# Block products for f tiles 8 to 11 of the first four batches, a later load, and a rewritten opening list

## The chip, the cores and the metric

The kernel runs on one core of one Trainium2 chip. The metric is the device time of one execution in microseconds; the kernel before was timed three times, and the median is 711.96 us. A separate execution was recorded by the hardware profiler, and all rows of the trace come from it.

## The reference

Eight batches of attention over 32 learned memory slots, followed by a gated feed-forward layer over all tokens:

```python
a = exp(phi - max(phi, -2)); a = a / (sum(a, -2) + 1e-9)       # over the sequence
k_m, v_m = einsum(a, k), einsum(a, v)                          # 32 slots a head
attn = softmax(q @ k_m.T / 8) @ v_m                            # batch, head, 576, 64
x = attn.transpose(0, 2, 1, 3).reshape(4608, 512)
out = (sigmoid(x @ w_gate) * (x @ w_val)) @ w_out              # d_ff = 1536
```

All data is float32, and the result is held to float32 accuracy.

## The kernel before

**Tiles.** A batch b has S = 576 rows. The hidden width 1536 is cut into NFT = 12 tiles f of 128. Rows are cut in two halves c: c = 0 has 256 rows, c = 1 has 256 rows and a tail of 64. The tails of two batches (a pair) are put together to one tile of 128 rows in the tiles `left`.

**Two terms a number.** Most matmuls are split: an operand is written as hi + lo, both in the format fp32r, and a product takes three matmuls, hi by hi, hi by lo and lo by hi. So each matrix product below is three instructions on TensorE.

**The gate.** x is never formed. `make_u` multiplies v_m by the weights (tiles `u_hi`, `u_lo`, for two f at a time; it takes 16 narrow matmuls for a pair of f), and `gate_of` multiplies these by the transposed attention (`at_hi`, `at_lo`): 12 matmuls for a half of a step, six for the gate and six for the value, of 256 columns in half 0 and of 320 in half 1. ScalarE makes the sigmoid from PSUM (`curve`, L218), VectorE multiplies (L830 or L1009).

**Eight block products.** In the first scheme (`gate_half`, `out_half`, `out_of`) a finished product of 256 rows is cut to hi and lo and multiplied by w_out: two row tiles by 512 columns, three terms, six matmuls of 512 columns for a step's half (b, f, c). Two f tiles make 12 such matmuls. This is a 2 by 2 block product by the eight multiplications of the definition.

**Seven block products.** In the second scheme (`first_half`, `second_half`, `seven`, `block_product`, `merge`) a pair k of f tiles is treated as a 2 by 2 block product by seven multiplications: sums of rows are made by VectorE (L1036, L1048, L1057, and three subtractions at L233 for the low terms), sums of the weights were prepared before and lie in DRAM as `block`s of seven pieces. It takes 7 products, three terms, 21 matmuls of 256 columns. `merge` puts the accumulators together by VectorE adds (L1149 to L1152, and L1159 with the rows parked earlier).

**Order of the work.** An `OPENING` list, written out by hand, says what each engine's queue gets, up to step 19. The names: `phi`, `kvm`, `kvt`, `q`, `gate`, `out`, `more` load by SyncE's queue; `amax`, `aexp` are the first softmax; `T`, `A` turn and copy its result; `K`, `B`, `t`, `V` make keys and values; `S`, `mx`, `ms`, `ex`, `nz`, `nm`, `tp`, `hi`, `lo` are scores, second softmax and its turned hi and lo; `sz`, `bt`, `ws`, `wb`, `wh`, `wl` convert weights; `U`, `uh`, `um`, `ul` are make_u; `G`, `sg`, `gm`, `gh`, `gl`, `O`, `E`, `row` are gates, outputs and parked rows; `W n` is n matmuls of the identity that nothing reads. `step` keeps this order on each engine.

Then a loop over `steps` runs the first scheme for batches 0 to 3 (`QUAD` = 4): f 0 to 3 of each batch, then f 4 to 7, then f 8 to 11, in turns of `TURN` = 4. A turn's result is parked in DRAM (`part`) and added by the next turn's end (`out_end`, L875). The loop also converts the last weights (`CONVERT`) and makes the blocks (`prepare`). Last, batches 4 to 7 run the second scheme throughout, 12 items (n, c, k) a batch, where n is a half of the f tiles. `beside_step` places the next batch's softmax, keys and turns between (`SIDE`). `row_of` fetches a parked row over ScalarE's queue; a wait of such a fetch holds what ScalarE has behind it.

## Time and profile before

| | |
|---|---|
| median of 3 runs | 711.96 us (710.71 to 712.0) |
| the profiled execution's own time | 714.1 us |
| its span, first to last instruction | 712.3 us |
| TensorE busy | 702.2 us, 6129 matmuls |
| VectorE busy | 500.5 us, 1028 instructions |
| ScalarE busy | 391.4 us |
| GpSimd busy | 37.4 us |
| mean granted TensorE clock | 0.995 |

A busy TensorE is not yet a TensorE at its peak: matmuls overlap, and a duration is longer than the distance to the next start. What a stream of matmuls costs is read from the starts.

### The profile page before, as it was taken

What the parts mean: (1) busy time and instruction counts of PE and PEld (TensorE: products, weight loads), DVE (VectorE), ACT (ScalarE), POOL (GpSimd) and SP (SyncE); (2) the same over time, 40 slices, a digit from 0 to 9 for tenths busy, and PEclk for the clock granted to TensorE, in tenths of its full rate; (3) what the DMA queues carried; (4) which work ended last, traced back from release to release, by engine and by line L of the source; (5) the groups of instructions that cost most, each with busy time, mean ns of one, the idle gap of its engine ahead of it and who ended that gap; (6) DMA issues with size and microseconds to landing.
All of it is one profiled execution on the core that took longest, in us unless ns stands there. A gap on an engine that the chain in (4) does not pass through costs nothing.

```text
span 712.3 us, 15350 instructions
## 1 busy us (share of the span) xinstructions
PE 702.2 (99%) x6129; PEld 617.8 (87%) x6129; DVE 500.5 (70%) x1028; ACT 391.4 (55%) x883; POOL 37.4 (5%) x73
## 2 busy tenths in 40 slices
PE   8999999999999999999999999999999999999996
PEld 6778888888888978889887989898998989999996
DVE  2688777543565747679475789777886788976766
ACT  5898796555465533344553665564645455544432
POOL 0000000000000002131000000000000000000001
PEclk9999999999999999999999999999999999999999
...
GB/s 346 412 258 337 236 227 148 161 207 262 275 186 207 249 78 315 138 292 303 332 188 324 104 199 220 297 339 42 251 187 190 236 93 313 107 307 44 260 116 99
DMA packets 46631, 158.27 MB, mean 222 GB/s; under 512 B 5472, under 2 KB 14176, under 8 KB 41440
## 3 DMA queue, kind: packets, MB, share of 16 engines
...
## 4 chain that ended last, share of the span: by engine, by line
PE 96%; DMA 2%; DVE 1%; issue 0%; ACT 0%; DVEq 0%; POOL 0%; SPq 0%; ACTq 0%; POOLq 0%
PE pu_t L243 58%; PE acc L243 38%; DMA part<-left 1%; DMA q<-in_qT_dram 1%; DVE row L1245 0%; DVE g_lo L233 0%; DVE left L875 0%; DVE x L1245 0%; DVEq L1519 0%; DVE x L1009 0%; ACT g L836 0%; ACT x L218 0%; SPq L229 0%; ACTq L229 0%; DVE x L1048 0%
## 5 line engine op out<-in xcount | busy, mean ns | idle before, releaser
L243 PE MATMUL pu_t<-at_hi,u_hi 128*128 128x256 f32 (+1 forms) x760 | 224.7, 296 | 0.0
L243 PE MATMUL pu_t<-at_lo,u_hi 128*128 128x256 f32 (+1 forms) x760 | 222.6, 293 | 0.0
L243 PE MATMUL pu_t<-at_hi,u_lo 128*128 128x256 f32 (+1 forms) x760 | 222.6, 293 | 0.0
L243 PEld LDWEIGHTS pu_t<-at_hi,u_hi 128*128 128x128 f32 x760 | 142.9, 188 | 6.2 <-issue 1.2
L243 PEld LDWEIGHTS pu_t<-at_lo,u_hi 128*128 128x128 f32 x760 | 142.7, 188 | 3.1
L243 PEld LDWEIGHTS pu_t<-at_hi,u_lo 128*128 128x128 f32 x760 | 142.6, 188 | 0.0
L243 PE MATMUL acc<-wo_hi,g 128*128 128x512 f32 x384 | 135.7, 399 | 0.7 <-ACT g L836 0.7
L243 PEld LDWEIGHTS acc<-wo_hi,g 128*128 128x128 f32 x384 | 72.1, 188 | 23.2 <-issue 9.2
L218 ACT ACTIVATE sg<-pu_t 128x256 f32<-128x256 f32 x94 | 38.4, 410 | 79.7 <-PE pu_t L243 76.2
L830 DVE TENSOR_TENSOR sg<-pu_t,sg 128x256 f32<-128x256 f32 (+1 forms) x94 | 42.3, 452 | 48.3 <-ACT sg L218 32.9
L243 PE MATMUL acc<-wo_lo,g 128*128 128x512 f32 x192 | 75.2, 392 | 0.0
L233 DVE TENSOR_TENSOR g_lo<-x,g_hi 128x128 fp32r<-128x128 f32 x145 | 66.4, 463 | 11.1 <-ACT g_hi L1059 10.1
L218 ACT ACTIVATE x<-pu_t 128x320 f32<-128x320 f32 (+1 forms) x96 | 39.1, 410 | 59.9 <-PE pu_t L243 59.5
L233 DVE TENSOR_TENSOR u_lo<-pu_t,u_hi 128x512 fp32r<-128x512 f32 x92 | 57.9, 682 | 16.2 <-ACT u_hi L738 16.1
L1009 DVE TENSOR_TENSOR x<-pu_t,x 128x320 f32<-128x320 f32 (+1 forms) x96 | 43.4, 453 | 32.6 <-ACT x L218 20.6
L836 ACT CAST g<-sg 128x256 fp32r<-128x256 f32 x96 | 38.9, 405 | 34.5 <-DVE sg L830 25.4
L738 ACT CAST u_hi<-pu_t 128x512 fp32r<-128x512 f32 x92 | 48.6, 592 | 14.2 <-PE pu_t L243 13.3
L233 DVE TENSOR_TENSOR g<-sg,g 128x256 fp32r<-128x256 f32 x96 | 39.6, 420 | 22.4 <-ACT g L836 22.1
L243 PE MATMUL pu_t<-wg,vT 64*32 64x512 f32 x736 | 49.6, 598 | 0.0
L1059 ACT CAST g_hi<-x 128x512 fp32r<-128x512 f32 x47 | 29.1, 619 | 24.0 <-DVE x L1057 24.0
L243 PE MATMUL acc<-wo_hi,g_hi 128*128 128x256 f32 x220 | 40.3, 282 | 0.0
L243 PEld LDWEIGHTS acc<-wo_lo,g 128*128 128x128 f32 x192 | 36.1, 188 | 4.6
...
## 6 DMA issues: line engine op xcount, KB each, us to landing
...
ring<-block POOLq DMA_DIRECT2D x8, 1792.0 KB, 8.7
wo_hi<-block POOLq DMA_DIRECT2D x7, 1792.0 KB, 8.2
wo_lo<-block POOLq DMA_DIRECT2D x7, 1792.0 KB, 9.2
...
```

Source lines behind the costliest of these rows:

```text
L218: last_act[0] = nc.scalar.activation(*args, **kw)
L233: return nc.vector.tensor_tensor(lo, x, hi.bitcast(F32), op=ALU.subtract)
L243: last_pe[0] = do(*args, **kw)
L738: nc.scalar.copy(U[b, fs[0]][0][:, r, :nf], pb[r])
L830: last_prod[0] = nc.vector.tensor_tensor(sg, val, sg, op=ALU.mult)
L836: nc.scalar.copy(ghi, prod[:, : 2 * P].rearrange("p (j x) -> p j x", j=2))
L1009: last_prod[0] = nc.vector.tensor_tensor(x[:, :n], val, x[:, :n], op=ALU.mult)
L1059: nc.scalar.copy(gh[:, 2:6], x[:, 1:5])
```

## The change

1. The loop over `steps` ends at f 7 (`END` = 8). F tiles 8 to 11 of batches 0 to 3 run the second scheme: pairs k = 2 and 1 of the upper half n = 1 (`LATE`), 4 items a batch, 16 in all, each in place of the first scheme's two steps' halves. The row parked by the first scheme is fetched (`part_fetch`) and added in `merge`. Tails go through `left_parts` and `left_seven`.
2. Blocks are made earlier: raw sums and differences by GpSimd instead of VectorE (`block_raw`, `block_sums`), placed by half step in `PREP`; blocks 4 and 5 are made in the place where they are used first (`late_parts`) and stored later (`block_keep`). Weights w_out of f 8 to 11 aren't cut to hi and lo any more; only their sums are. Block stores go over SyncE's queue, not GpSimd's. A block is loaded by two transfers, one for hi and one for lo.
3. Keys and values of batch 6 (the seventh) are loaded in item 6 of batch 4's work, not beside the memory of batch 5.
4. The opening list is another one, and a name with ' runs its copy on the other engine (`copy`: ScalarE and VectorE change places). `W` counts 81 in all with the 24 ahead of the list, where there were 102.

The diff, cut to its core:

```diff
+END = 8
+LATE = (2, 1)
+LOW_AHEAD = {(0, 1): 4}
-PREP = [1] * 8 + [2, 1] * 6 + [1] * 20
+PREP = {
+    0: ("raw", 0), 1: ("sums", 0), 3: ("parts", 0), 4: ("raw", 1), 5: ("sums", 5), 6: ("sums", 1), 9: ("parts", 1), 10: ("parts", 5, 0), 11: ("parts", 5, 1),
+    19: ("sums", 4), 21: ("parts", 4, 0), 22: ("parts", 4, 1), 24: ("raw", 2), 25: ("put", 5), 26: ("sums", 2), 27: ("raw", 3), 28: ("sums", 3), 31: ("parts", 2), 33: ("put", 4), 35: ("parts", 3),
+}
-    21: [(8, 2)], 22: [(9, 0)], 24: [(9, 2)], 25: [(10, 0)], 27: [(10, 2)], 28: [(11, 0)], 30: [(11, 2)],
+CONVERT = {20: (10, 2), 21: (9, 0), 22: (11, 2), 24: (10, 0), 26: (8, 2), 28: (11, 0), 29: (9, 2)}
...
-phi 0; gate 0; kvm 0 0; kvt 0; kvm 0 1; amax 0; aexp 0; W 24; T 0 0; T 0 2; T 0 1; A 0 2; A 0 0; phi 1;
-q 0 0; A 0 1; W 5; K 0 0; gate 1; sz 0 1; q 0 1; out 0; gate 3; sz 0 0;  W 6; K 0 1; kvm 1 0;
-Z 0; B 0; kvt 1; amax 1; gate 2; phi 2; W 6; t 0; kvm 1 1; bt 0 1; V 0 0; aexp 1;  W 4; S 0 0;
-bt 0 0; V 0 1; Z 1; T 1 1; mx 0 0; T 1 2; sz 1; ms 0 0; W 14; S 0 1; A 1 1;  ws 0; bt 1; T 1 0;
-q 1 0; ex 0 0; mx 0 1; U 0 0; q 1 1; A 1 0; out 1; A 1 2; ms 0 1; uh 0 0; nz 0 0; ex 0 1; W 10; um 0 0;
-nm 0 0; sz 3; nz 0 1; tp 0 0; nm 0 1; hi 0 0; W 7; tp 0 1; ul 0 0; lo 0 0; K 1 0;  hi 0 1; wb 0;
...
+gate 0; sz 0 0; phi 0; kvm 0 0; kvt 0; kvm 0 1; amax 0; aexp 0; W 31; Z 0; T 0 0; A' 0 0; T 0 1; T 0 2;
+W 9; A' 0 2; A' 0 1; sz 0 1; K 0 0; phi 1; amax 1; q 0 0; gate 1; q 0 1; W 16; K 0 1; B 0; t 0; aexp 1;
+V' 0 0; bt 0 0; Z 1; bt 0 1; S 0 0; mx 0 0; V' 0 1; T 1 1; T 1 2; T 1 0; S 0 1; ms 0 0; sz 1; bt 1;
+U 0 0; W 1; mx 0 1; ms 0 1; A 1 1; A 1 0; A 1 2; ex 0 0; nz 0 0; uh 0 0; um 0 0; nm 0 0; ex 0 1; nz 0 1;
+gate 3; sz 3; tp 0 0; hi' 0 0; ul 0 0; lo 0 0; kvm 1 0; kvt 1; K 1 0; G 0 1 0; G 0 0 0; phi 2; amax 2;
+nm 0 1; out 0; ws 0; wb 0; bt 3; tp 0 1; aexp 2; sg 0 1 0; hi' 0 1; sg 0 0 0; lo 0 1; kvm 1 1; K 1 1;
+B 1; gm 0 1 0; wh 0; wl 0; gm 0 0 0; gate 2; q 1 0; q 1 1; T 2 1; T 2 0; t 1; G 0 0 1; sz 2; A 2 1;
...
+E 0 7 0 0; fetch 0 1; again 1; row 0 7 0; O 0 6 1; O 0 7 1; E 0 7 0 1; E 0 7 1 1; ul 1 6; E 0 7 1 0;
+row 0 7 2; row 0 7 1; row 0 7 3; V 4 0; V 4 1; sz 8; bt 8;
...
+    def copy(to, x, act=True):
+        (nc.scalar.copy if act != swapped[0] else nc.vector.tensor_copy)(to, x)
...
+    def block_sums(k):
+        work = works[k]
+        raw = work[:, : 2 * DM].rearrange("p (f h x) -> p f h x", f=2, h=2)
+        sums = work[:, 2 * DM :].rearrange("p (j x) -> p j x", j=4)
+        sub = lambda to, *of: nc.gpsimd.tensor_tensor(to, *of, op=ALU.subtract)
+        sub(sums[:, 1], raw[:, 0, 1], raw[:, 0, 0])
+        sub(sums[:, 0], raw[:, 0, 1], raw[:, 1, 1])
+        sub(sums[:, 2], raw[:, 1, 1], sums[:, 1])
+        sub(sums[:, 3], raw[:, 1, 0], sums[:, 2])
+    def block_raw(k):
+        work = works[k] = att([P, SF, 512], "kvm0" if k == 3 else "kvm1").rearrange("p c x -> p (c x)")
+        hi, lo = (w[:, 2 * k : 2 * k + 2, :] for w in wos)
+        nc.gpsimd.tensor_tensor(work[:, : 2 * DM].rearrange("p (f x) -> p f x", f=2), hi, lo, op=ALU.add)
...
+    def load_block(n, k, queue="stream"):
+        for i in range(2):
+            move(ring(k, i).bitcast(F32), blocks_of[n * PAIRS + k][:, i], queue)
+    def pairs(b):
+        return LATE if b < QUAD else tuple(range(PAIRS))
...
-    turns = [(b, f0, f0 + TURN) for f0 in range(0, NFT, TURN) for b in range(QUAD)]
+    turns = [(b, f0, f0 + TURN) for f0 in range(0, END, TURN) for b in range(QUAD)]
...
-        load_next(b + 1)
+        if b == QUAD + 1:
+            load_phi(b + 1)
+        else:
+            load_next(b + 1)
...
+        if late:
+            s = i % low_at
+            if s == 0 and b + 1 < QUAD:
+                again(b + 1)
+            if s in (1, 3):
+                part_fetch(b, c)
+            if b == 1 and s == 2:
+                load_block(0, 0)
+            if i == 10:
+                load_kv(QUAD + 1)
...
+        if (b, s) == (QUAD, 6):
+            load_kv(b + 2)
...
+        if late:
+            if c == 0 and last:
+                if b in (0, 1):
+                    scores(QUAD, b)
+                if b + 1 == QUAD:
+                    memory(QUAD + 1)
+                    make_u(QUAD, [0, 1], [2, 3])
+                else:
+                    make_u(b + 1, *([2 * (PAIRS + j), 2 * (PAIRS + j) + 1] for j in LATE))
```

## Rows read from the trace of the kernel before

**Rows 1.** The page, parts 1 and 4: busy time, and the chain by engine.
```profile
PE 702.2 (99%) x6129; PEld 617.8 (87%) x6129; DVE 500.5 (70%) x1028; ACT 391.4 (55%) x883; POOL 37.4 (5%) x73
...
PE 96%; DMA 2%; DVE 1%; issue 0%; ACT 0%; DVEq 0%; POOL 0%; SPq 0%; ACTq 0%; POOLq 0%
```

**Rows 2.** Windows: stretch, length, busy of five engines, clock, DMA share, GB/s.
```profile
20.00:40.00 20.00, 19.91 (x234) 15.67 (x232) 14.59 (x25) 18.88 (x30) 0.00 (x0) 0.93 0.99 403
...
180.00:200.00 20.00, 19.31 (x137) 17.29 (x122) 9.93 (x19) 9.94 (x23) 1.78 (x3) 1.00 0.71 249
...
600.00:620.00 20.00, 20.00 (x182) 18.54 (x181) 19.59 (x43) 10.50 (x25) 0.28 (x1) 1.00 0.42 136
```

**Rows 3.** Timeline of TensorE in the first scheme: start, length, line, operands, count.
```profile
340.83 0.28 PE L243 MATMUL pu_t<-at_hi,u_hi 128*128 128x256 f32 x1
...
342.25 0.40 PE L243 MATMUL acc<-wo_hi,g 128*128 128x512 f32 x1
...
343.62 0.31 PE L243 MATMUL pu_t<-at_hi,u_hi 128*128 128x320 f32 x1
...
346.88 1.95 PE L243 MATMUL pu_t<-wg,vT 64*32 64x512 f32 x32
348.76 0.50 PE L243 MATMUL acc<-wo_hi,g 128*128 128x512 f32 x1
...
351.66 0.28 PE L243 MATMUL pu_t<-at_hi,u_hi 128*128 128x256 f32 x1
```

**Rows 4.** Timeline of TensorE in the second scheme, one item.
```profile
600.74 0.31 PE L243 MATMUL pu_t<-at_hi,u_hi 128*128 128x320 f32 x1
...
604.26 0.40 PE L243 MATMUL acc<-wo_lo,g_hi 128*128 128x256 f32 x2
...
606.74 0.28 PE L243 MATMUL pu_t<-at_hi,u_hi 128*128 128x256 f32 x1
```

**Rows 5.** Groups of VectorE, 415.8 to 543 us: busy, mean ns, idle before.
```profile
L233 DVE TENSOR_TENSOR g_lo<-x,g_hi 128x512 fp32r<-128x512 f32 x18 | 12.4, 690 | 3.2 <-ACT g_hi L1059 3.1
L233 DVE TENSOR_TENSOR u_lo<-pu_t,u_hi 128x512 fp32r<-128x512 f32 x19 | 11.9, 680 | 2.9 <-ACT u_hi L738 2.9
L1009 DVE TENSOR_TENSOR x<-pu_t,x 128x320 f32<-128x320 f32 x18 | 8.7, 482 | 2.9 <-ACT x L218 1.4 <-PE pu_t L243 1.4
L1048 DVE TENSOR_TENSOR x<-x,x 128x256 f32<-128x256 f32 x18 | 7.6, 422 | 0.3
...
L1057 DVE TENSOR_TENSOR x<-x,x 128x128 f32<-128x128 f32 x18 | 5.2, 288 | 0.3
...
L1150 DVE TENSOR_TENSOR row<-row,acc 128x512 f32<-128x512 f32 x6 | 4.1, 681 | 0.2
```

**Rows 6.** Timeline of TensorE in the opening.
```profile
1.37 7.56 PE L243 MATMUL acc<-ident 128*128 128x256 bf16 x48 [1.37 <-POOL ident masks.py:199]
...
17.39 1.97 PE L243 MATMUL acc<-kT,q 128*128 128x64 f32 x16 [1.21 <-DMA q<-in_qT_dram]
...
33.12 0.38 PE L243 MATMUL pu_t<-at_hi,u_hi 128*128 128x256 f32 x1
```

**Rows 7.** Groups of TensorE over the span: the matmuls that nothing reads.
```profile
L243 PE MATMUL acc<-ident 128*128 128x256 bf16 x102 | 16.2, 322 | 1.4 <-POOL ident masks.py:199 1.4
```

**Rows 8.** Timeline of ScalarE in the opening.
```profile
20.79 1.21 ACT L260 ACTIVATE wg<-wg,over 128x1024 f32<-128x1024 int8 x1 [2.23 <-DMA wg<-in_wgv_dram]
22.03 1.44 ACT L261 ACTIVATE wg<-wg,under 128x1024 int16<-128x1024 f32 x1
...
25.35 0.60 ACT L218 ACTIVATE e<-e 128x512 f32<-128x512 f32 x1
...
31.81 1.07 ACT L759 CAST u_lo<-acc 128x512 fp32r<-128x512 f32 x2
```

**Rows 9.** Windows at the clock's changes, columns as in rows 2.
```profile
19.45:22.86 3.41, 3.41 (x19) 2.55 (x18) 1.34 (x2) 2.04 (x2) 0.00 (x0) 0.50 1.02 422
```

**Rows 10.** Timeline of ScalarE behind the opening.
```profile
191.74 0.40 ACT L836 CAST g<-sg 128x256 fp32r<-128x256 f32 x1 [6.23 <-DMA part<-left]
```

**Rows 11.** Groups of GpSimd over the span.
```profile
L1245 POOL TENSOR_TENSOR row<-row,x 128x256 f32<-128x256 f32 x1 | 1.2, 1237 | 0.0
L1245 POOL TENSOR_TENSOR row<-x,wo_hi 128x256 f32<-128x256 f32 x1 | 0.7, 738 | 31.1 <-ACT x L1245 31.1
```

**Rows 12.** The page, part 6: size, median us from issue to landing.
```profile
ring<-block POOLq DMA_DIRECT2D x8, 1792.0 KB, 8.7
```

More of the change, by code (lines that the diff above doesn't have):

```diff
@@ L285, in load_jobs @@
             f, k = jobs[0]
[L286 removed]
+            if (k == 2 and f >= NE and not rings) or len(waiting) == 2:
                 break
@@ L768, in left_room @@
         return left_rooms[k]
-    SPARE = {k: (1, 2) if k < 7 else (3, 5) for k in range(12)}
-    steps_at = [0]
     def left_of(pair, f):
@@ new lines, in late_parts @@
+    def late_parts(k, half):
+        work, slot = works[k], k - PAIRS
+        hi, lo = ring(slot, 0), ring(slot, 1)
+        pieces = ((slice(4, 7), slice(5 * 256, 8 * 256)),) if half else ((slice(0, 1), slice(0, 256)), (slice(1, 4), slice(DM, DM + 3 * 256)))
+        with behind():
+            for js, xs in pieces:
+                nc.scalar.copy(hi[:, js], work[:, xs].rearrange("p (j x) -> p j x", x=256))
+            for js, xs in pieces:
+                rest(lo[:, js], work[:, xs].rearrange("p (j x) -> p j x", x=256), hi[:, js])
+        if half:
+            del works[k]
@@ L1024, in left_fetch @@
     def left_fetch(pair, n):
-        for k in range(PAIRS):
+        for k in pairs(2 * pair):
             f = (n * PAIRS + k) * 2
@@ new lines, in attn_moe_kernel @@
+    low = tb.tile([P, 2, 2, 256], F32R, name="u3_hi").bitcast(F32).rearrange("p r f x -> p (r f x)")
+    rows_of = tb.tile([P, 2, 2, 256], F32R, name="u3_lo").bitcast(F32)
+    rows_low.extend(rows_of[:, i] for i in range(2))
+    tb.tile([P, DM], F32, name="row", bufs=2)
+    small_tile()
+    lasts.append(None)
+    for o in (0, 256):
+        lasts.append(low[:, o : o + 256].rearrange("p (h f x) -> p h f x", h=2, f=2))
+    blocks_at = {b: [1] if b < QUAD else range(NBLK) for b in range(B)}
@@ L1431, in attn_moe_kernel @@
+    order = [(b, n, c, k) for b in range(B) for n in blocks_at[b] for c in (1, 0) for k in pairs(b)]
+    low_at = 2 * len(LATE)
+    n_low = QUAD * low_at
+    held, side = None, new_side(QUAD, QUAD + 1)
     for i, (b, n, c, k) in enumerate(order):
-        s = i % (2 * NBLK * PAIRS)
+        first, last, late = k == pairs(b)[0], k == pairs(b)[-1], b < QUAD
+        s = (i - n_low) % (2 * NBLK * PAIRS)
         more = b + 1 < B
-        if s == 0:
+        if late:
[3 more added lines that the diff above has]
+            if s in (1, 3):
+                if i == n_low // 2 + 1:
+                    rows_low.clear()
+                part_fetch(b, c)
+            if b == 1 and s == 2:
+                load_block(0, 0)
+            if b == 1 and s == 0:
+                move(low[:, 512:], left_sum[0])
+                left_sum[0] = low[:, 512:]
+            if i == 10:
+                load_kv(QUAD + 1)
+        elif s == 0:
+            if b == QUAD:
+                lasts.clear()
@@ L1442, in attn_moe_kernel @@
         first_half(b, f, c)
-        beside_step(SIDE, 2 * s)
+        blocks_step(2 * (END * QUAD - DONE + i))
+        beside_step(plan, of_half)
         now = second_half(b, f, c, k)
-        if b % 2 and (c, k) == LEFT_AT[1]:
+        if b % 2 and c == 0 and first:
             left_seven(b // 2, n)
-        ahead = AHEAD.get((c, k), 0) if held else 0
+        ahead = (LOW_AHEAD if late else AHEAD).get((c, k), 0) if held else 0
         if ahead:
             seven(*held, SEVEN[:ahead])
-        if more and (n, c, k) in SC_AT:
-            scores(b + 1, SC_AT[n, c, k])
```

391 lines of the change are left out of this document (184 added, 207 removed).

## The prediction

> **What bounds the kernel now.** I read the page first, then the windows of 20 us, then TensorE's timeline. TensorE is busy 702.2 of 712.3 us and holds 96% of the chain that ended last; DMA has 2% of it, VectorE 1% [rows 1]. So the other engines matter only where they make TensorE wait, and the windows name few such places: the first 40 us, and one between 180 and 200 us with 19.31 us busy of 20 [rows 2]. Everywhere else the time is the number of matmuls by the distance of their starts. VectorE isn't idle beside that: in one late window it is busy 19.59 of 20 us, while TensorE still shows 20.00 [rows 2]. That is the picture to keep: a stream of matmuls without gaps, and a second engine close behind it where the second scheme runs.
>
> The distance of starts has to be read between groups, since durations overlap. Six wide matmuls (512 columns) take 1.37 us from the first to the next gate's start (342.25 to 343.62); twelve in a row behind a make_u take 2.90 us (348.76 to 351.66); twelve gate matmuls of 256 columns take 1.42 us (340.83 to 342.25), and 32 narrow ones of make_u 1.88 us [rows 3]. In the second scheme 24 gate matmuls of 320 columns take 3.52 us and the 21 block products of an item 2.48 us (604.26 to 606.74), 118 ns each [rows 4].
>
> **Part 1, seven for eight.** It replaces 12 wide matmuls by 21 of 256 columns in each of 4 batches by 2 halves by 2 pairs, 16 items. The old price lies between 2 x 1.37 = 2.74 and 2.90 us [rows 3], the new one is 2.48 us [rows 4]. So 0.26 to 0.42 us an item, 4.2 to 6.7 us in all. I take 0.33, the middle, since old groups stood both alone and in runs: **5.3 us less**. Gates and make_u are as many as before. The tails are even: per pair 12 matmuls of 512 columns go, and 24 of 256 come.
>
> A rule speaks against this step. The Trainium skill (TensorE: Matmul & The Clock Gate, Back-to-back issue gap) gives sustained distances of about 81 ns at 128 columns and 131 ns at 512. By that 12 wide ones would cost 1.57 us and 21 at some 98 ns (an estimate between its two figures) 2.06 us, so the change would add 0.49 us an item, 7.8 us in all. The trace doesn't agree: 1.37 us for six is 228 ns each, and the sum goes by the rows.
>
> What comes with it on VectorE: an item has two products (0.48 or 0.42 us), three instructions of 128 columns (0.29), two of 256 (0.42) and one of 512 (0.69), 3.3 us, so 53 us for 16 [rows 5]. Eight merges of three adds at 0.68, one at 0.42 and two more at 0.68 for the parked row are 3.8 us each, 31 us. The low parts of u are 16 by 0.68, 11 us. The softmax of batch 4, the first maximum of batch 5, the tails and two blocks' low parts I estimate at 19 us, from 0.68 us for 512 columns scaled by their sizes. Together 113 us of durations; back to back they overlap (19 of 0.680 would be 12.9 us, busy 11.9 [rows 5]), so some 104 us. TensorE's plan for the stage is 8 x (3.52 + 2.48) + 8 x (2.84 + 2.48) = 91 us, with 4 x 1.9 for make_u, 6 for tails and an estimated 5 for keys, turns and scores 109 us. VectorE would be 95% busy. The nearest row is the window at 600 us: 98% busy and no idle TensorE [rows 2], which gives a lower bound of nothing.
>
> Two things are tighter here than there. make_u of the next batch stands directly ahead of the item that uses it, with three block products (9 x 0.118 = 1.1 us) and the second pair's 0.9 us as cover, while two high copies on ScalarE and two low ones on VectorE (2 x 0.68) must end; and merges come every second item instead of every third. If a merge's 3.8 us is covered by two gates alone (2.8 us), 1.0 us is left over, 8 us for eight: the upper bound. I take **1.2 us more**, a quarter or so for each of the four batch changes, since the row of 98% is the nearer.
>
> **Part 2, blocks earlier.** VectorE loses the sums and the cuts of eight weight halves, GpSimd gets them: 24 subtractions of 256 columns at 0.74 to 1.24 us [rows 11], 18 to 30 us, and four adds of 1024, an estimate of 3 to 5 us each by the same rows, spread over some 120 us in which GpSimd has little else [rows 1]. Nothing waits for them but the high copies on ScalarE half a step or more later, and the weight loads issued behind them on GpSimd's queue; a load is used two conversions later, so I count this as nothing, and 2 us if one load is late. What is late next is the conversion in step 20, which came in step 21 before: its words can't be loaded until the last conversion of the opening (`bt 8`, the list's last word now) has read the buffer. ScalarE's wait of 6.23 us for a parked row there left the one gap of the stage [rows 2, 10]. It can grow by the conversion and shrink by an earlier store; bounds minus 0.7 (that window's idle time) and plus 3, I take **0.3 more**. Block 1 of the lower half is loaded only when the last item of batch 3 has used its place; its first use comes two items later: 0.9 us wait-free margin at best, as 3.5 + 2.5 + 3.5 = 9.5 us stand against 8.7 us to land [rows 4, 12]. Bounds 0 and 2 us, I take **0.3 more**. SyncE's queue gets the block stores and the fetches of parked rows one item ahead of their merge; behind a fetch that waits stand the merge's own stores and the next batch's attention, which has four items. Counted as nothing; if a fetch were late by a transfer, the merge bound above covers it.
>
> **Part 3, the seventh batch's load.** It moves 2.3 MB from one TensorE-bound stretch to another. Nothing, as DMA is on 2% of the chain [rows 1].
>
> **Part 4, the opening.** Before the first gate at 33.12 us TensorE runs the unread matmuls and waits; from 20 to 40 us DMA is 99% busy and ScalarE 18.88 of 20 us [rows 2, 6]. The bytes ahead of the first scores are the same (only the first weights and the first phi change places), so the scores can't start much before 17.39 us, where they waited for q [rows 6]. Then the weights of gate 1 land at 20.79, and their conversion holds ScalarE to 23.5 [rows 8]. By the new order three copies (an estimate of 0.5 each), the exponential (0.60), two u copies (1.07, as `ul`), the second exponential (0.75 for 640 columns by the first's 0.60 for 512), the conversion `sz 3` (1.21 + 1.44) and `ul` (1.07) follow [rows 8]: 31.3 us. Before, `ul` ended at 31.81 + 1.07 = 32.9 [rows 8], since two more conversions and two copies stood ahead of it. So the first gate comes some 1.5 us earlier. Behind it the new order sets `ws 0`, `aexp 2`, the table load, two sigmoids and `B 1` ahead of `t 1` on ScalarE, an estimated 6 us in which TensorE has two gates of half 0, `tp`, `K 1 1` and two turns, some 5 us: a wait of 1 to 1.5 us takes the place of what was won. One thing more: only one unread matmul stands between 14.5 us and the first gate (41 before). The clock fell to 0.50 (1.2 GHz) at 19.45 us, behind scores after a wait, and rose again at 22.86 with 14 unread matmuls in between [rows 9]. Without these it can stay low into the first gates; a stretch of 3.4 us at half speed costs up to 1.7 us. That the clock needs activity to be released, as the Trainium skill has it (TensorE: Matmul & The Clock Gate, What's actually happening), agrees with that row. All 102 unread matmuls have 16.2 us of busy time [rows 7]; the 21 that go give nothing by themselves, as they filled waits. Bounds minus 2 and plus 3.5 us; I take **nothing**.
>
> **Sum.** 5.3 less, 1.2 + 0.3 + 0.3 more: 3.5 us less. Against its own time the profiled execution would go from 714.1 (712.3 of span and 1.8 around it) to 710.6 us. It lies 2.1 above the median; from the median 711.96 the forecast is **708.5 us**.
>
> **The rivals.**
> *The opening wins as well*: the first gate's 1.5 us stays, and the late stage has no waits. 711.96 - 5.3 - 1.5 = 705.2. For it: VectorE at 98% without a gap. Against: the wait for `t 1`. Chance 0.17.
> *The gain is eaten*: waits at batch changes, the clock and the gap at step 20 add up to 4 to 6 us: 711 to 713. Chance 0.12.
> *VectorE bounds the late stage*, slower: each merge leaves 1.0 us uncovered: 8.0 + 0.6 - 5.3 = 3.3 us more, 715.3. It decides from 0.66 us a merge (5.3 / 8) on. For it: 95% by my count, every second item a merge. Against: the window at 600 us. Chance 0.13.
> *The narrow products start slower in the new place*: at the 147 ns of the gates of half 1 (3.52 / 24 [rows 4]) 21 cost 3.08 us, 0.26 more than 2.82, so 4.2 us more and 716.2; it decides from 134 ns on. Against it: 118 ns in all of the later stage. Chance 0.02. The page named above would make it so too.
>
> **How the numbers follow.** My forecast, 706 to 710.5, has 0.56. A change of 0.2%, 1.4 us, is about what can be told from none. Faster is the forecast and the first rival, 0.73; no change 0.12; slower 0.15. The range 704 to 713 holds all but the slower cases' bulk and a little below.
>
> **What would show it.** Right: matmuls 6129 - 192 - 24 + 336 + 48 - 21 = 6276; 2.5 us for 21 products in the new stage; TensorE's busy windows near 20.00 from 230 to 380 us; the batch-4 work beginning some 5 us earlier relative to the first gate. Wrong, each by itself: TensorE waiting for `u_lo` or for a merge's add in the late stage; the first gate after 33.1 us or at clock 0.50; a gap over 2 us near step 20. The prediction fails if these waits exceed 4 us, or if the new list lets TensorE drop more than 2 us of waiting ahead of the first gates.

## The result, and the profile after

The changed kernel takes 716.27 us (median of 13 runs, 714.43 to 720.17), the kernel before 712.00 in 13 runs beside it: a ratio of 1.0059, 95% interval [1.0043, 1.0076]. It is slower by about 4.3 us; the forecast was 708.5, in a range that ended at 713.0.

The profiled execution is the slowest of the 13, 720.17 us. Why it is, the windows show. First the page of the changed kernel, parts 1 and 4, to set beside [rows 1]:

```profile
PE 703.6 (98%) x6276; PEld 625.5 (87%) x6276; DVE 541.1 (75%) x1144; ACT 390.9 (54%) x869; POOL 59.5 (8%) x91
...
PE 83%; DVE 7%; ACT 4%; DMA 3%; issue 1%; SPq 0%; DVEq 0%; POOL 0%; ACTq 0%; POOLq 0%
```

The 6276 matmuls are those of the forecast. But TensorE's share of the chain that ended last falls from 96% to 83%: other engines now decide the time at some places. Windows of the same execution (columns as in [rows 2]) say where:

```profile
20.00:36.00 16.00, 15.60 (x119) 10.71 (x123) 9.44 (x19) 10.96 (x16) 0.00 (x0) 0.50 1.01 412
...
100.00:120.00 20.00, 18.88 (x162) 15.54 (x161) 15.60 (x29) 10.31 (x20) 0.00 (x0) 1.00 0.69 244
140.00:160.00 20.00, 19.27 (x137) 15.91 (x122) 10.78 (x26) 7.31 (x19) 0.00 (x0) 1.00 0.77 276
220.00:240.00 20.00, 18.17 (x105) 15.53 (x104) 12.64 (x22) 10.72 (x23) 9.43 (x10) 1.00 0.91 322
340.00:360.00 20.00, 18.68 (x167) 16.79 (x166) 17.48 (x42) 12.79 (x29) 0.00 (x0) 1.00 0.72 246
```

The clock was at 0.50 (1.2 GHz) from 19.1 to 36.2 us, 17 us; before it was 3.4 us [rows 9]. And TensorE has gaps at four later places: 100 to 120, 140 to 160, 220 to 240 and 340 to 360 us. The same windows of the kernel before have none:

```profile
100.00:120.00 20.00, 20.00 (x144) 16.58 (x138) 16.52 (x26) 13.99 (x30) 0.00 (x0) 1.00 0.29 106
...
140.00:160.00 20.00, 20.00 (x143) 16.76 (x128) 9.57 (x21) 10.90 (x28) 0.00 (x0) 1.00 0.63 218
...
220.00:240.00 20.00, 20.00 (x144) 16.79 (x143) 11.02 (x21) 10.30 (x22) 0.54 (x1) 1.00 0.53 191
...
340.00:360.00 20.00, 20.00 (x144) 16.78 (x143) 9.32 (x19) 10.88 (x22) 0.00 (x0) 1.00 0.81 299
```

A second profile of the same program (run after_again, 716.81 us) kept the gaps and lost the long stretch:

```profile
20.00:36.00 16.00, 15.49 (x193) 12.07 (x192) 13.48 (x24) 13.91 (x21) 0.00 (x0) 0.89 1.01 415
...
100.00:120.00 20.00, 18.88 (x173) 15.50 (x179) 15.19 (x28) 11.01 (x20) 0.00 (x0) 1.00 0.73 260
140.00:160.00 20.00, 18.69 (x124) 15.91 (x123) 10.40 (x26) 6.36 (x15) 0.00 (x0) 1.00 0.64 243
220.00:240.00 20.00, 18.17 (x107) 15.08 (x113) 14.79 (x25) 12.01 (x27) 9.07 (x11) 1.00 0.83 290
340.00:360.00 20.00, 18.69 (x166) 16.74 (x165) 16.57 (x40) 14.12 (x32) 0.00 (x0) 1.00 0.70 234
```

Here the clock is at half for 3.4 us, as in the profile of before, and the first gate comes at 30.89 us, 2.2 us *earlier* than before [rows 6]. (Some 0.7 us of that is a matter of order: five matmuls of `tp 0 1`, which ran ahead of the gate, now stand behind it.) Yet the kernel ends later: its last matmul of `ring` starts at 709.24 us, that of before at 705.73. After_again, then before:

```profile
30.89 0.39 PE L249 MATMUL pu_t<-at_hi,u_hi 128*128 128x256 f32 x1
...
709.24 0.28 PE L249 MATMUL pu_t<-ring,g_lo 128*128 128x256 f32 x1
```

```profile
705.73 0.28 PE L243 MATMUL pu_t<-ring,g_lo 128*128 128x256 f32 x1
```

So at equal clock the change costs 3.5 us, and all of it, with what was won at the first gate and what the products give, is lost behind that gate. TensorE's waits in this execution, longest first:

```profile
PE pu_t L249 <- ACT sg L218: 1.7, 2, 1.1
...
PE pu_t L249 <- DMA at_lo<-at: 1.3, 1, 1.3
PE acc L249 <- DVE g L239: 1.0, 1, 1.0
PE pu_t L249 <- DVE u_lo L239: 0.9, 1, 0.9
...
PE acc L249 <- DVE g_lo L239: 0.5, 1, 0.5
```

The products themselves do what was forecast. TensorE's timeline of after_again, one item of the new stage: the first of 21 products, and the first matmul behind them.

```profile
314.89 0.40 PE L249 MATMUL pu_t<-ring,g_hi 128*128 128x256 f32 x2
...
317.37 0.28 PE L249 MATMUL pu_t<-wo_hi,g_hi 128*128 128x256 f32 x1
```

2.48 us for 21, 118 ns each, as in the later stage [rows 4].

### The profile page after: what moved, and what is told of

Read it like the earlier page. It is cut to its first block, busy times and chain, and to the rows that moved or that the text cites. A ratio compares the mean times of both kernels' runs of the same rounds, so it can differ in the third digit from the quotient of the medians.

```text
span 718.4 us, 15854 instructions
## 1 busy us (share of the span) xinstructions
PE 703.6 (98%) x6276; PEld 625.5 (87%) x6276; DVE 541.1 (75%) x1144; ACT 390.9 (54%) x869; POOL 59.5 (8%) x91
## 4 chain that ended last, share of the span: by engine, by line
PE 83%; DVE 7%; ACT 4%; DMA 3%; issue 1%; SPq 0%; DVEq 0%; POOL 0%; ACTq 0%; POOLq 0%
PE pu_t L249 52%; PE acc L249 32%; DVE u_lo L239 1%; DMA at_lo<-at 1%; DMA at<-at_lo 1%; DMA ph<-in_phiT_dram 1%; ACT L218 1%; DVE g_lo L239 1%; DMA part<-row 1%; DVE sg L834 1%; DVE nmx L423 0%; ACT ph L218 0%; ACT sg L218 0%; ACT wg L267 0%; DVE at_lo L239 0%
## 5 line engine op out<-in xcount | busy, mean ns | idle before, releaser
L239 DVE TENSOR_TENSOR g_lo<-x,g_hi 128x128 fp32r<-128x128 f32 (+2 forms) x193 | 88.3, 463 | 12.5 <-ACT g_hi L1087 11.7
L249 PE MATMUL acc<-wo_hi,g 128*128 128x512 f32 x256 | 89.9, 401 | 1.3 <-DVE g L239 1.0
L249 PE MATMUL acc<-wo_hi,g_hi 128*128 128x256 f32 x276 | 78.0, 282 | 0.0
L249 PE MATMUL acc<-wo_lo,g_hi 128*128 128x256 f32 x276 | 76.9, 279 | 0.0
L249 PE MATMUL acc<-wo_hi,g_lo 128*128 128x256 f32 x276 | 76.9, 279 | 0.0
L249 PEld LDWEIGHTS acc<-wo_hi,g 128*128 128x128 f32 x256 | 48.0, 188 | 15.8 <-issue 3.7
L249 PE MATMUL acc<-ring,g_hi 128*128 128x256 f32 x332 | 60.3, 282 | 0.0
L249 PEld LDWEIGHTS acc<-ring,g_hi 128*128 128x128 f32 x332 | 50.5, 188 | 9.4 <-issue 6.9
L249 PEld LDWEIGHTS acc<-wo_hi,g_hi 128*128 128x128 f32 x276 | 51.9, 188 | 6.7 <-issue 6.7
L249 PEld LDWEIGHTS acc<-wo_hi,g_lo 128*128 128x128 f32 x276 | 51.9, 188 | 0.0
L249 PEld LDWEIGHTS acc<-wo_lo,g_hi 128*128 128x128 f32 x276 | 51.8, 188 | 0.0
```

Source lines behind the costliest of these rows:

```text
L239: return nc.vector.tensor_tensor(lo, x, hi.bitcast(F32), op=ALU.subtract)
L249: last_pe[0] = do(*args, **kw)
```

## The experiments

Two theories at first. T1: the new opening list costs the most, and the rest of the change comes out about even. T2: the new stage with its conversions and VectorE work costs the most. Each kernel below is the changed kernel with an edit, unless it says otherwise; its median stands against that of the kernel before on the same chip.

**1. The list alone, the rest alone.** old_opening takes the list `OPENING` of the kernel before into the changed kernel; new_opening takes the new list, with the copies that it sends to other engines, into the kernel before.

```diff
-gate 0; sz 0 0; phi 0; kvm 0 0; kvt 0; kvm 0 1; amax 0; aexp 0; W 31; Z 0; T 0 0; A' 0 0; T 0 1; T 0 2;
+phi 0; gate 0; kvm 0 0; kvt 0; kvm 0 1; amax 0; aexp 0; W 24; T 0 0; T 0 2; T 0 1; A 0 2; A 0 0; phi 1;
...
```

old_opening: 

> The changed kernel with the opening list of the kernel before; seven for eight and the later load stay. T1 (the new opening list costs the most: first gate 3.4 us later, later waits of PE at 113 and 153 us): 709 to 712 us, ratio to before 0.996 to 1.000, first gate near 33.1 us, clock at half for under 4 us. T2 (the new stage with its conversions and its VectorE work costs the most, the opening about nothing): 714 to 717 us, ratio 1.003 to 1.007. Both: 6276 + 19 = 6295 or so matmuls, since the old list has 78 unread ones for 57 or so.

new_opening: 

> The kernel before with the new opening list and its copies on other engines; eight block products everywhere, the seventh batch loaded where it was. T1: 715 to 719 us, ratio 1.005 to 1.010, first gate near 36.5 us. T2: 711 to 713.5 us, ratio 0.998 to 1.002, whatever the first gate does.

old_opening 710.84 us, ratio 0.9994 [0.9981, 1.0006]; new_opening 716.69, ratio 1.0083 [1.0058, 1.0108]; after_again 716.99, 1.0088 [1.0061, 1.0115]. T2 falls: the list alone, without one of the new products, is as slow as the whole change. By the medians the list costs 4.6 us (716.69 - 712.08) and the rest gives 1.2 (712.08 - 710.84); the interval of the first is 4.1 to 7.7 us, that of the second reaches from 1.4 us less to 0.4 us more. T1's time held; its first gate near 36.5 us did not, as new_opening's profile has it at 30.62.

With the same list in both, one can match matmul with matmul. Against before, old_opening is 0.21 us late at the products behind the list (192.76 and 192.97) and 2.59 us early behind the new stage (395.12 and 392.53): 2.8 us won. The four matmuls, before's two first:

```profile
192.76 0.62 PE L243 MATMUL acc<-wo_hi,g 128*128 128x512 f32 x2
...
395.12 0.40 PE L243 MATMUL acc<-wo_hi,g_hi 128*128 128x256 f32 x2
```

```profile
192.97 0.62 PE L251 MATMUL acc<-wo_hi,g 128*128 128x512 f32 x2
...
392.53 0.28 PE L251 MATMUL acc<-wo_hi,g_hi 128*128 128x256 f32 x1
```

TensorE's waits there were 0.30, 0.30, 0.61 and 1.06 us, 2.3 in all (each is the distance of two starts less the usual one, so it is a little more than the idle time in a view of waits). So the products gave 5.1 us (5.3 forecast), and the new stage's waits took 2.3 back (1.2 forecast).

Matched in the same way, new_opening stands 2.6 us behind the kernel before at 194 us and 3.9 us at the end. So a third of its loss falls behind the list, mainly in two waits, 0.77 us at 217 and 1.00 at 394.

after_again: 

> The changed kernel once more, for a second profiled execution: its first showed the clock at half from 19.08 to 36.15 us and a mean clock under that of its other runs. If the long stretch at half clock is what the new list always does: half clock for 10 to 17 us again and first gate at 35 to 37 us. If it was one execution's: half clock for under 5 us, first gate at 32 to 34 us, and the profile 2 to 4 us shorter. Time in both cases 715 to 717, ratio 1.004 to 1.008.

The long stretch was one execution's, but not a rare one. Over 19 runs of the changed kernel the mean granted clock is 0.9948, over 114 of the kernel before 0.9975. Runs at 0.997 took 714.4 to 715.8 us, those at 0.986 and 0.987 took 720.1 to 722.1. A run at 0.986 has 15.8 us more at half clock than one at 0.997 (0.011 x 2 x 718) and is some 5 us longer, a third of a microsecond for each. The mean differs by 3.9 us at half clock (0.0027 x 2 x 716), so by this estimate the clock explains some 1.3 us of the loss. The profiles point the same way: in the nine with the old list no stretch behind the scores is longer than 3.4 us, and three of the nine with the new list have 17 us (after, ex_later, exp_later).

**2. The unread matmuls put back.**

```diff
-V' 0 0; bt 0 0; Z 1; bt 0 1; S 0 0; mx 0 0; V' 0 1; T 1 1; T 1 2; T 1 0; S 0 1; ms 0 0; sz 1; bt 1;
-U 0 0; W 1; mx 0 1; ms 0 1; A 1 1; A 1 0; A 1 2; ex 0 0; nz 0 0; uh 0 0; um 0 0; nm 0 0; ex 0 1; nz 0 1;
-gate 3; sz 3; tp 0 0; hi' 0 0; ul 0 0; lo 0 0; kvm 1 0; kvt 1; K 1 0; G 0 1 0; G 0 0 0; phi 2; amax 2;
+V' 0 0; bt 0 0; Z 1; bt 0 1; S 0 0; mx 0 0; V' 0 1; T 1 1; T 1 2; T 1 0; W 14; S 0 1; ms 0 0; sz 1; bt 1;
+U 0 0; W 1; mx 0 1; ms 0 1; A 1 1; A 1 0; A 1 2; ex 0 0; nz 0 0; uh 0 0; W 10; um 0 0; nm 0 0; ex 0 1; nz 0 1;
+gate 3; sz 3; W 7; tp 0 0; hi' 0 0; ul 0 0; lo 0 0; kvm 1 0; kvt 1; K 1 0; G 0 1 0; G 0 0 0; phi 2; amax 2;
```

opening_unread: 

> The changed kernel with three groups of unread matmuls (14 ahead of the second half's scores, 10 ahead of the first um, 7 ahead of the first tp) put back where the list before had them. If the first gate is late because TensorE's clock fell to half while it had little to do (T1a): the granted clock is 1.0 from some 24 us on, the first gate comes at 33 to 34.5 us, and the time falls by 1.5 to 3 us, to 713 to 715. If it is late because the chain of loads and conversions ahead of it is later (T1b): first gate at 36 to 37 us whatever the clock, 716 to 717 us.

715.22 us, ratio 1.0045 [1.0023, 1.0066], mean clock 0.9967; in its profile the clock was at half for 6.8 us, and the first gate came at 34.47. The time fell by 1.1 to 1.8 us, which is at the edge of T1a's numbers; but after_again has its first gate at 30.89 without these matmuls, so a late first gate is not what the list costs. With the two waits of the next experiment mended (mended_unread) they gave nothing: 

> The changed kernel with both waits of its list mended as in the run with ex 3 moved (714.46) and the 31 unread matmuls put back at their three places. If the stretches at half clock cost about a third of their length, and the unread matmuls shorten them: the mean granted clock over the runs rises from 0.9953 to 0.997 to 0.998, and the time falls by 0.7 to 1.3 us, to 713.2 to 713.8. If the clock does not follow them, 714.3 to 715. Neither reaches the old list's 710.84, since at equal clock the list still has its smaller waits at 60 to 80 us and the waits at 220 to 232 us behind it.

714.59 us, ratio 1.0036 [1.0019, 1.0053], beside 714.46 without; mean clock 0.9961 beside 0.9953. One thing did differ: none of these 22 runs has a mean clock under 0.993, and 10 of the 60 with the new list and without the unread matmuls have 0.985 to 0.988 (exp_later, which has a second stretch at half, is left aside). So the unread matmuls may keep the longest stretches away; the medians don't show it, and what keeps the clock lower in the other runs is not settled.

**3. Two waits inside the list.** The timeline of ScalarE in after_again at the first of them, and of TensorE at both:

```profile
105.14 0.38 ACT L218 ACTIVATE sg<-pu_t 128x256 f32<-128x256 f32 x1 [0.78 <-PE pu_t L249]
105.54 1.28 ACT L218 ACT_TABLE_LOAD   x1
106.84 1.17 ACT L218 ACTIVATE e<-e 128x1152 f32<-128x1152 f32 x1
...
108.80 1.28 ACT L218 ACT_TABLE_LOAD   x1
110.10 0.44 ACT L218 ACTIVATE sg<-pu_t 128x320 f32<-128x320 f32 x1
```

```profile
110.59 0.38 PE L249 MATMUL pu_t<-at_hi,u_hi 128*128 128x256 f32 x1 [1.12 <-ACT sg L218]
...
150.89 0.41 PE L249 MATMUL pu_t<-at_lo,u_hi 128*128 128x320 f32 x1 [1.31 <-DMA at_lo<-at]
```

Between two sigmoids of one gate tile the new list sets `ex 3`. ScalarE loads its tables for the exponential and back, 1.28 us each, and TensorE stands until the second sigmoid frees its bank. In the kernel before, the sigmoids around that exponential stood at 96.71 and 107.75, one pair of loads served it and `aexp 4`, and TensorE had no wait there. The other: `keep 1` stands five entries ahead of `again 0`, which loads into the place that `keep 1` stores. The chain shows the store landing and the load behind it:

```profile
136.96 6.23 DMA at<-at_lo
...
143.26 7.59 DMA at_lo<-at
```

two_waits moves `keep 1` ahead, directly behind `keep 2`, and `aexp 3` beside `ex 2`; ex_later moves `keep 1` alike, and `ex 3` behind both sigmoids, with the outputs `O 1 3 1` behind these gates. The diff is that of ex_later:

```diff
-row 1 3 1; S 3 0; tr 3 0; gl 2 0 1; S 3 1; tr 3 1; mx 3; ms 3; O 1 3 1; G 2 1 0; E 1 3 1 1; sg 2 1 0;
-row 1 3 0; phi 4; more 3; gm 2 1 0; ex 3; gh 2 1 0; E 1 3 1 0; U 2 2; G 2 1 1; gl 2 0 0; O 2 0 0;
-uh' 2 2; sg 2 1 1; ul 2 2; G 2 2 0; sg 2 2 0; nz 3; gm 2 2 0; nm 3; gh 2 2 0; gm 2 1 1; gl 2 2 0;
+row 1 3 1; S 3 0; tr 3 0; gl 2 0 1; S 3 1; tr 3 1; mx 3; ms 3; G 2 1 0; sg 2 1 0; G 2 1 1; sg 2 1 1; O 1 3 1; E 1 3 1 1;
+row 1 3 0; phi 4; more 3; gm 2 1 0; ex 3; gh 2 1 0; E 1 3 1 0; U 2 2; gl 2 0 0; O 2 0 0;
+uh' 2 2; ul 2 2; G 2 2 0; sg 2 2 0; nz 3; gm 2 2 0; nm 3; gh 2 2 0; gm 2 1 1; gl 2 2 0;
...
-gh' 2 3 1; O 2 1 1; gm 2 2 1; gl 2 3 1; sg 2 3 0; gm 2 3 0; keep 2; kvm 4 0; more 4; row 1 3 2; gl 2 1 0;
+gh' 2 3 1; O 2 1 1; gm 2 2 1; gl 2 3 1; sg 2 3 0; gm 2 3 0; keep 2; keep 1; kvm 4 0; more 4; row 1 3 2; gl 2 1 0;
...
-ul 0 4; sg 3 2 0; gm 3 2 0; gh 3 2 0; wb 5; gl 3 2 0; wh' 5; row 2 3 1; keep 1; row 2 3 2; kvt 4;
+ul 0 4; sg 3 2 0; gm 3 2 0; gh 3 2 0; wb 5; gl 3 2 0; wh' 5; row 2 3 1; row 2 3 2; kvt 4;
```

two_waits: 

> The changed kernel with two entries of its opening list moved: aexp 3 directly ahead of ex 2, so that ScalarE loads its tables once for both, and keep 1 from behind row 2 3 1 to directly behind keep 2, so that the store it issues has landed long before the load of again 0 overwrites the buffer. T1 in its second form (the new list costs by two waits of PE, 1.29 us for sg at 109 us and 1.3 to 1.5 us for at_lo at 149 us, and by the clock for the rest): both waits gone, 2.0 to 2.7 us less than the changed kernel, 713.5 to 715, ratio 1.002 to 1.005. Rival (PE only waits elsewhere, because ScalarE's work there is late anyway): less than 0.8 us less, 715.5 to 717.

ex_later: 

> The changed kernel with keep 1 directly behind keep 2, aexp 3 back in its place (its exponentials had stood beside those of ex 2 at 73 us all along, so the move in the run before moved nothing), and ex 3 behind both sigmoids of the gate tile at 105 us, with O 1 3 1 and its ends moved behind those gates: PE then has 6 wide products, U 2 2, 6 wide products and 12 gate matmuls, some 5.3 us, for the 4.7 us in which ScalarE loads tables, computes e and loads tables again. Theory: the wait of 1.29 us for sg there goes, and the reload's of 1.48 too: 2.4 to 2.9 us less than the changed kernel, 713.3 to 714.2, ratio 1.002 to 1.004. Rival (PE waits for g instead, since both gates' products stand behind e on ScalarE): less than 0.5 us less than with the reload mended alone (715.36), 715 to 715.6.

two_waits 715.36 us, ratio 1.0055 [1.0035, 1.0076]; ex_later 714.46, ratio 1.0033 [1.0016, 1.0050]. In the first the reload's wait is gone and the other stands unmoved (1.28 us, behind the matmul of 107.47): I had moved the wrong exponential: `aexp 3` stood beside `ex 2` at 73 us all along, and the one that holds TensorE is `ex 3`. In the second both are gone, but for 0.2 us at 113.8. The windows of both (two_waits in the first fence, ex_later in the second):

```profile
100.00:120.00 20.00, 18.88 (x177) 14.94 (x160) 16.81 (x31) 10.42 (x20) 0.00 (x0) 1.00 0.87 319
140.00:160.00 20.00, 20.00 (x134) 17.37 (x133) 9.27 (x24) 7.84 (x19) 0.00 (x0) 1.00 0.43 162
```

```profile
100.00:120.00 20.00, 19.73 (x170) 16.27 (x169) 15.77 (x27) 9.93 (x19) 0.00 (x0) 1.00 0.68 248
140.00:160.00 20.00, 20.00 (x136) 17.45 (x135) 10.93 (x26) 8.22 (x21) 0.00 (x0) 1.00 0.62 215
```

So these two waits are 1.8 to 2.5 us of the list's 4.6 (716.27 and 716.99 to 714.46, on different chips).

**4. The gap at 220 us.** In the changed kernel ScalarE's queue stands at 216 to 220 us until a store of rows has landed, since the fetch of the next rows into the same place is issued by ScalarE.

```diff
-    def row_of(b, t, queue="rows"):
+    def row_of(b, t, queue="batch"):
```

rows_by_sync: 

> The changed kernel with the fetches of the parked rows on SyncE's queue instead of ScalarE's. Theory: ScalarE's queue was held at 220 us until a store of the same rows had landed (4.4 us), and sg, g and left behind it; the 0.75, 0.38 and 1.19 us of PE at 220, 225 and 228 us go, 1.5 to 2.3 us less than the changed kernel, 714 to 715. Rival (VectorE's and ScalarE's conversions of the third block are the backlog and the fetch only stood in front): the waits move by less than 0.8 us in sum, 715.5 to 717.

716.38 us, ratio 1.0069 [1.0044, 1.0093]. The rival holds: the waits of 0.75, 0.38 and 1.19 us became 1.76, 0.65 and 0.48. With the old list the same program has no gap there; its store lands in 2.1 us instead of 4.3, and the DMA engines had been idle for 2.8 us (209.0 to 211.8), while with the new list they stay busy throughout (the view of DMA issues, as in [rows 12], for 214 to 222 us of after_again, then for 209 to 216 us of old_opening):

```profile
part<-row SPq DMA_DIRECT2D x2, 256.0 KB, 4.3
```

```profile
part<-row SPq DMA_DIRECT2D x2, 256.0 KB, 2.1
```

In new_opening the window from 220 to 240 us has TensorE busy for 20.00 us, and a wait of 0.77 us is left ahead of it. So most of the gap needs the new list and the new stage together.

**5. The gap at 186 us with the old list.** old_opening has a wait of 1.88 us behind the matmul of 186.75 (the kernel before has one of 0.85 us some 2.5 us of work later, in the same step). Its chain, and the timelines of VectorE and GpSimd:

```profile
178.76 3.34 DVE wg L351
...
182.73 4.56 DMA words<-in_wo_dram
...
187.64 0.75 ACT kvm L268
188.39 0.33 ACT sg L220
```

```profile
178.68 3.42 DVE L351 SCALAR_TENSOR_TENSOR wg<-words,wg 128x1024 int32<-128x1024 int32 x1
...
178.58 2.42 POOL L971 TENSOR_TENSOR kvm<-wo_hi,wo_lo 128x1024 f32<-128x1024 f32 x1 [177.27 <-DMA row<-part]
```

The word operation takes 3.42 us; its four others take 1.21 to 1.22. It begins 0.1 us behind GpSimd's first addition. Until it ends the words can't be overwritten (their next load is issued 0.6 to 0.7 us behind its end here, in the kernel before and in raw_by_vector), so the next words are loaded late, ScalarE's conversion waits for them, and the sigmoid behind it holds TensorE. Two runs tried to move the addition to later halves of the plan and left it beside the word operation (3.45 us in both): GpSimd still took it up when the same transfer had landed. They tell nothing of the theory:

raw_later: 

> The old list with the new stage, and in it the first addition of weight parts on GpSimd (1024 columns) half a step later, its differences behind it too. Theory: with the old list PE's wait of 1.88 us at 186.75 came because that addition (178.58 to 181.00) and VectorE's word operation (178.68 to 182.09, 3.42 us beside 1.22 without a neighbour) held each other up, so that the words buffer came free, and the load of the next words was issued, 2.2 us late. Then the word operation takes 1.22 us again and the wait falls under 0.5 us: 1.4 to 1.9 us less than with the old list alone (710.84), 708.8 to 709.6, ratio 0.995 to 0.998. Rival (the load itself, 4.56 us, and what is queued ahead of it, is the length of the chain): the wait stays over 1.2 us and the time at 710 to 711.

raw_two_later: 

> The old list with the new stage, and GpSimd's additions and differences for the first two blocks two halves later, so that the first addition stands behind the load of words on GpSimd's own queue (in the run before it had kept its place at 177.87, and VectorE's word operation its 3.44 us). Theory: the word operation takes 1.22 us, the load of words is issued some 2.2 us earlier relative to PE, and the wait of 1.74 us at 186 falls under 0.5: 1.2 to 1.7 us less than the version before (710.50), 708.7 to 709.4, ratio 0.995 to 0.997. Rival (the load's landing of 4.5 us sets it all the same): wait over 1.2 us, 710 to 711.

710.50 us, ratio 0.9982 [0.9970, 0.9993], and 711.68, ratio 0.9991 [0.9978, 1.0004]; waits of 1.74 and 1.67 us. The third gives it to VectorE:

```diff
-        nc.gpsimd.tensor_tensor(work[:, : 2 * DM].rearrange("p (f x) -> p f x", f=2), hi, lo, op=ALU.add)
+        (nc.gpsimd if k else nc.vector).tensor_tensor(work[:, : 2 * DM].rearrange("p (f x) -> p f x", f=2), hi, lo, op=ALU.add)
```

raw_by_vector: 

> The old list with the new stage, and the addition of weight parts for the first block alone on VectorE in place of GpSimd, since moving it within GpSimd's work had left it at its place twice (178.26 us, beside the word operation of 3.46 us). Theory (VectorE and GpSimd hold each other up there): the word operation takes 1.22 us; even with the addition's own 1.2 us ahead of it the load of words is issued 1 us earlier or more, and PE's wait at 186 falls from 1.67 to 1.88 us to under 0.9: 708.9 to 710.1, ratio 0.995 to 0.998. Rival (the load's landing sets the wait): it stays over 1.4 us, 710.5 to 711.5.

709.01 us, ratio 0.9964 [0.9950, 0.9978]: faster than the kernel before by 2.6 us and than the changed one by some 7. Its timeline of VectorE, and TensorE's window that had 18.28 us with old_opening:

```profile
180.38 1.22 DVE L351 SCALAR_TENSOR_TENSOR wg<-words,wg 128x1024 int32<-128x1024 int32 x1
181.52 1.22 DVE L971 TENSOR_TENSOR kvm<-wo_hi,wo_lo 128x1024 f32<-128x1024 f32 x1
```

```profile
180.00:200.00 20.00, 20.00 (x152) 17.37 (x141) 12.86 (x22) 11.72 (x25) 5.99 (x9) 1.00 0.86 310
```

The addition and the word operation now take 2.36 us on one engine (180.38 to 182.74), less than the 3.42 that they took side by side on two, and the wait is gone. The theory is shown for the old list. With the new one the two don't meet: the word operation stands at 188.90 in after_again and takes 1.21 us.

**6. The waits of the new stage.** At the change from batch 2 to batch 3 ScalarE has a block of 4 us: a table load of 1.28, `e` 1.17 and two `ph` of 0.76; the next U's high copies stand behind it, and `u_lo` behind them. VectorE has the largest feature (1.34) and a merge there. Four edits of the side plan:

```diff
-SIDE_1 = {0: ('max',), 5: ('amax',), 7: ('exp',), 9: ('sum',), 10: ('turn', 'T0'), 14: ('T1', 'T2')}
+SIDE_1 = {0: ('max',), 5: ('amax',), 8: ('exp',), 9: ('sum',), 10: ('turn', 'T0'), 14: ('T1', 'T2')}
```

exp_later: 

> The changed kernel with the exponentials of the fifth and sixth batch one half step later beside the new stage, so that their table load, e and ph stand behind the conversions of the next batch's first U instead of ahead of them. Theory: the waits of 0.6 and 1.05 us of PE at the change of batches (353.49 and 357.81 us in the first profile) go, 1.0 to 1.7 us less than the changed kernel, 714.5 to 716. Rival (VectorE is the bound of that stage, as its 95% by count suggests, and gives the wait at the next merge): less than 0.5 us less.

old_opening_both (that, the edit of experiment 4, and the old list): 

> The changed kernel with the opening list of the kernel before and with both edits at once, the fetches of rows on SyncE's queue and the exponentials half a step later. If the terms add: 1.2 to 1.7 us under the version with the old list alone (710.84), since the wait at 186 us there is one for words and not for rows: 709 to 709.8, ratio 0.995 to 0.998, a version faster than both. Rival (each edit only moves its wait): 710.5 to 711.5, ratio 0.998 to 1.000.

exp_earlier (halves 3 and 5 for `amax` and `exp`, with the old list): 

> The old list with the new stage, and in it the largest feature and the exponentials of the side plan two halves earlier (halves 3 and 5 for 5 and 7), away from the merge at 338 to 347 us and from the change of batches. Theory (the place matters: at half 7 they meet the merge's five additions and the first U of the next batch): the waits of 0.61 and 1.06 us go, 1.0 to 1.7 us less than with the old list alone, 709.1 to 709.9. Rival (both engines have no slack left anywhere in these two batches, as the move to half 8 showed with 5.3 us at 360 to 366): the waits come back elsewhere with 1.5 us or more, 710.8 to 714.

amax_earlier (half 4 for `amax`, on raw_by_vector): 

> As the run beside it, and the largest feature of the side plan one half earlier (half 4 for 5), so that its 1.34 us of VectorE no longer stand in front of the merge's additions at 338 to 344 us; the exponentials stay at half 7. Theory (VectorE's work makes the 0.61 us at 344, as leaving out the parked rows showed): that wait goes, 0.4 to 0.7 us less than the run beside it, unless the 1.06 us behind it grow by as much, as they did when the rows were left out (2.27 us). Rival: no difference that the runs can tell.

exp_later 724.29 us, ratio 1.0166 [1.0137, 1.0195]; old_opening_both 716.07, 1.0054 [1.0032, 1.0075]; exp_earlier 717.45, 1.0064 [1.0044, 1.0084]; amax_earlier 711.11, 0.9995 [0.9985, 1.0006]. No move helped. With `exp` half a step later the 1.06 us are gone, and two waits of 1.96 and 3.30 us come 12 us behind; two halves earlier, one of 4.89 us. TensorE's waits in both (exp_later from 355 to 380 us, exp_earlier from 330 to 356):

```profile
PE acc L249 <- DVE g_lo L239: 3.6, 2, 3.1
PE acc L249 <- ACT g_hi L1087: 1.7, 1, 1.7
```

```profile
PE acc L251 <- ACT g_hi L1089: 4.7, 1, 4.7
```

In exp_later `sum`, `turn` and the merge's additions all fall behind the late `e` and stand ahead of `g_lo` on VectorE. With `amax` half a step earlier there are waits of 0.86 and 2.48 us behind 337 and 347 us (raw_by_vector has 0.62 and 1.01 there).

Waiting is not all that these moves cost. In all four profiles the granted clock also fell to 0.50 during or at the end of these waits: from 373.5 to 380.4 us in exp_later, 363.8 to 370.6 in old_opening_both, 343.3 to 350.2 in exp_earlier and 349.3 to 352.7 in amax_earlier. In old_opening and raw_by_vector it stays at 1.00 there. Windows of exp_earlier, then of old_opening:

```profile
344.00:350.00 6.00, 5.64 (x25) 5.41 (x26) 5.13 (x9) 2.42 (x4) 0.00 (x0) 0.50 0.71 286
```

```profile
343.00:350.00 7.00, 5.65 (x61) 3.75 (x59) 5.80 (x16) 6.90 (x15) 0.00 (x0) 1.00 0.92 334
```

Matched with old_opening, exp_earlier loses 5.7 us between 337 and 372 us, where its waits are only 3.2 us more (4.89 against 0.61 and 1.06). The other 2.5 us come in the stretch at half clock.

no_parked_rows is old_opening with work taken from VectorE alone: it leaves out the additions of the parked rows in batches 0 to 3.

```diff
-            nc.vector.tensor_tensor(halves_of_r, halves_of_r, lasting(i), op=ALU.add)
+            if b >= QUAD:
+                nc.vector.tensor_tensor(halves_of_r, halves_of_r, lasting(i), op=ALU.add)
```

> The old list with the new stage; left out are the eight pairs... of additions on VectorE that add the parked rows of the first eight f tiles to a merged row of batches 0 to 3 (16 additions of 512 columns, 0.67 us each), so that the rows of those batches lack the first part of their sum. If VectorE's work bounds the new stage: the waits of 0.30, 0.30, 0.61 and 1.06 us at 294, 322, 344 and 348 us fall to under 0.8 in sum, 1.5 to 2 us less than with the old list alone (710.84). If ScalarE's block of table loads, e and ph (4.0 us from 343.8) sets them: only the wait at 344 falls, 0.3 to 0.8 us less, and the 1.06 us behind it stays or grows.

709.83 us, ratio 0.9975 [0.9960, 0.9991], beside 710.84 and 0.9994 for old_opening, which has the rows (on another chip); matched matmul by matmul the stage is 1.0 us shorter. The waits of 0.30, 0.30 and 0.61 us are gone, so they were VectorE's; the last one grew from 1.06 to 2.27 us: there ScalarE's block sets the time, and TensorE only reaches it earlier.

## Why the prediction was wrong

**The step that failed is Part 4**, "Bounds minus 2 and plus 3.5 us; I take nothing". What it worked out held: at equal clock the first gate came 2.2 to 2.5 us earlier (30.89 and 30.62, against 33.12), "some 1.5 us" by the sum, and TensorE's wait behind it was small (0.3 us at 40). (The rows of that sum add up to 31.1 us and not 31.3, and the margin of block 1 in Part 2 to 0.8 us and not 0.9; neither changes the forecast.) But the sum stopped at the first gates, and the list fixes the order of all four engines to about 180 us. Its cost lay in the part that I hadn't walked: an exponential between two sigmoids (1.29 us), a store set too close ahead of the load into its place (1.3 to 1.5), and smaller waits (at 60 to 80 us new_opening's distances of starts are some 1.0 us longer than before's). Only the first two were tested by an edit; they are 1.8 to 2.5 us together. The clock was named, with "up to 1.7 us"; one execution had 17 us at half, and the runs' mean puts the price at some 1.3. The 4.6 us lie outside the bounds, since the bounds were those of 40 us and the step was one of 180; some of them fell even later (217 and 394 us).

**Part 1 held**: 5.1 us against 5.3. The rule of the Trainium skill that was weighed there (TensorE: Matmul & The Clock Gate, Back-to-back issue gap) would have made the products dearer; the trace doesn't agree here either, 118 ns for each of 21 in the new stage bears out the rows. The late stage's waits were 2.3 us, not 1.2. VectorE was one cause (the three waits of 1.2 us that no_parked_rows took away); the other, ScalarE's block of exponentials at a change of batches, was on none of the lists, because I counted engines' busy time and not what stands ahead of `u_hi`.

**Part 2** put GpSimd's sums at nothing: "Nothing waits for them but the high copies on ScalarE". With the old list VectorE did. The word operation began 0.1 us behind GpSimd's addition and took 3.42 us, 2.3 to the end of that addition and 1.1 more, nearly its own 1.2. The Trainium skill (SBUF — State Buffer, Who interferes with whom) states that a VectorE instruction with two inputs in SBUF contends with a GpSimd instruction that reads SBUF, and calls the ports that the two share an exclusive lock. The trace agrees. One product `g` of 0.42 us took 3.37 (226.08, old_opening) where an addition of 2.39 us and two differences ran, while `sg` with an input in PSUM kept its 0.4 us beside a difference (184.41). I priced the engine that got the work, and not its neighbour. With the old list that step cost 1.0 us more than before, and raw_by_vector got it back with 0.9 on top. In the changed kernel, with the new list, VectorE's operations were stretched by 4 us in all (after_again, eight operations from 202 to 268 us), and no run tells what that cost TensorE.

**Part 3** held: no wait for the seventh batch's keys and values; behind 400 us the waits are the same in all kernels to 0.3 us.

The nearest rival was that the gain is eaten, 711 to 713: it named the clock, the batch changes and step 20, all three of them real, and no wait inside the list. Two other rivals came nearer by their numbers alone, 715.3 and 716.2: but the products started every 118 ns, and the new stage waited 2.3 us and not 8. Without Part 4 the kernel takes 710.84 us, and the forecast of 708.5 was 2.3 us too low: 1.1 us of the late stage's waits, 0.4 at step 20 (1.0, against 0.6 with block 1's load, which cost nothing) and 0.2 of the products are the terms that were off, 1.7 in all; the other 0.6 is less than the interval of that median.

What stays open: why the clock is lower with the new list, with the unread matmuls back too, what the rest of the list's 4.6 us is beside the two waits mended and the estimate for the clock, and what keeps the 220 us gap open in rows_by_sync, beyond that VectorE and ScalarE have the third block's conversions there.
